# Batch 1's landmark sums around batch 0's z, the A of batch 0's last tokens ahead of B's scaling, batch 2's scores a slot later, and GpSimd's work in another order

## The chip, the cores and the metric

The kernel runs on one core of a Trainium2 chip. The metric is the device time of one execution in microseconds; the median of three executions of the kernel before is 260.71 us (260.47, 260.71 and 262.13).

## The reference

Nystrom attention over 8 batches of 8 heads (576 tokens of 64 values), followed by a SiLU feed-forward layer:

```python
m = 32
scale = 1.0 / np.sqrt(D)
q_lm = q.reshape(B, H, m, S // m, D).mean(axis=3)
k_lm = k.reshape(B, H, m, S // m, D).mean(axis=3)
...
A = sm(q, k_lm)
Bm = sm(q_lm, k_lm)
C = sm(q_lm, k)
Z = Bm.transpose(0, 1, 3, 2) / (norm_1(Bm) * norm_inf(Bm) + 1e-06)
for _ in range(6):
    Z = 2 * Z - Z @ Bm @ Z
return A @ Z @ C @ v
...
h = x @ w_in          # x: 4608 x 512, w_in: 512 x 2048
g = h * (1.0 / (1.0 + np.exp(-h)))
return g @ w_out      # w_out: 2048 x 512
```

Here `sm(a, b)` is a softmax over the last axis of `scale * a @ b.T`, and `norm_1` and `norm_inf` stand for the two matrix norms in the original (written there with numpy's `linalg.norm`).

## The kernel before

Batches run one after the other in a loop over `b`, and each has 16 slots `s`. In a slot TensorE computes one up-projection pair (`l1_mm`, tile `hps`: 256 of the 2048 hidden features for half the tokens), ScalarE applies Silu to it (`l1_act`, tile `gT`), and TensorE works off some down-projection products (`l2_mm`, tile `ops`); how many is written by hand in the lists `CNT` (batches 0 to 2) and `REST`. Between these the attention of the next batch is prepared, so that the feed-forward layer of one batch hides the attention of the following one. The order of every instruction is the order of the Python text: there is no scheduler, and each engine (TensorE PE, VectorE DVE, ScalarE ACT, GpSimd POOL, and the DMA queue SP) works its instructions strictly in that order.

The attention of a batch goes through these steps, each with its helper:

- `load_qk` and `load_v` issue the loads from GpSimd's queue (tiles `nat` with four parts, k and q of heads 0 to 3 and of heads 4 to 7, and `v`). Weights `w_in` and `w_out` are loaded on the same queue.
- Landmark sums over 18 tokens each: for batches 0 and 1 as 18 accumulating products with the identity (`landmarks_pe`, tile `lmp`, evacuated by ScalarE in `landmarks_out`); from batch 2 on by GpSimd (`landmarks_pool`, L223 to L238: five additions for a half of the heads). The result `lmn` is transposed on VectorE (`lm_t`, tile `lmc`).
- `transpose_qk` turns q and k on VectorE (1.25 us each, four for each batch).
- Scores of B and C (`b_scores`, `c_scores`, tiles `bb` and `scp`), their maxima on VectorE, exponentials on ScalarE; B's scaling (`f_mm`, `b_scale`, `f_out`) and then the Newton steps, each a product on TensorE (`ns_mm`) and an update on VectorE (`ns_step`); `x_out` is the last update.
- `w_mm` and `w_out` form C times v, `z_mm` and `z_out` multiply with z, and `m_unit` or `m_pair` multiply the result with `w_in` (tile `mb`), one "unit" for 512 of the 2048 features. So the up-projection of a batch uses `mb` and the transposed A (`AT`) alone.
- The A scores: in batches 0 and 1 chunk by chunk (`a_scores`, `a_exp`, `a_norm`, whose multiplication is GpSimd's, and `a_transpose`); from batch 2 on for the whole batch (`a_pair`: 32 products into `sa`, two transposes and two maxima on VectorE, a subtraction of the maximum on GpSimd, tile `xs`), normalised in `a_sum` and `a_mul`, turned in `a_back`.

The exponential and Silu need different ScalarE tables, so that each switch (`table`) costs a load of 1.28 us.

Where the change lies: before the loop the z of batch 0 is formed (`a.z_mm`, `a.z_out`), then 18 landmark products of batch 1 are issued in two pieces around unit 0. In slots 0 to 4 of batch 0 the rest of batch 1's attention is started and A of batch 0's last tokens is computed; in slots 5 to 15 (`r = s - d`, with `d = 2`) come batch 1's Newton steps, z and units. In batch 1 itself `d` says in which slot batch 2's A scores are made: slot `d` starts batch 2's landmark transpose and `a_pair`, slot `d + 1` the scores of B and C, slot `d + 2` their exponentials, and so on to the units in slots `d + 11` and `d + 13`. `l1_tail` copies a batch's last 64 tokens in front of the next one's, on GpSimd.

PSUM is split in pools: two slots for `hps`, `scp`, `sa` and pairs of units (`ps2`), two for `ops` (`pso1`), one for `bb` and `lmp` (`psn1`), one more (`psa1`). A tile of a pool waits until the tile that had its place has been read.

Of the kernel before, what the change touches and what calls it, by code (L numbers as in the profile page):

```python
# [9 lines left out]
BF = mybir.dt.bfloat16  # L10
# [33 lines left out]
def kernel(  # L44
# [38 lines left out]
    def ps2(nm):  # L83
        return psh.tile([128, 2, 512], FP, tag="h", name=nm)
# [159 lines left out]
    class Att:  # L244
# [376 lines left out]
        def a_pair(self):  # L621
            self.a_first()
            for i in range(2):
                self.a_scores(i)
            for i in range(2):
                nc.vector.transpose(  # L626
                    out=self.xs[:, i],
                    in_=self.sa[i][:, :, 0:HF].rearrange("p r (t n) -> p r t n", n=L))
            for i in range(2):
                nc.vector.tensor_reduce(out=self.nm[:, i], in_=self.xs[:, i], op=OP.max,  # L630
                                        axis=AX.X, negate=True)
                nc.gpsimd.tensor_tensor(  # L632
                    out=self.xs[:, i], in0=self.xs[:, i],
                    in1=self.nm[:, i].unsqueeze(3).to_broadcast((128, 2, SEG // 2, L)),
                    op=OP.add)
# [198 lines left out]
    def l2_add(b, *blocks):  # L834
        for i in blocks:
# [3 lines left out]


    CNT = {0: [0, 0, 0, 0, 4, 4, 2, 4, 4, 4, 2, 2, 2, 2, 1, 1],
           1: [2, 2, 6, 4, 10, 8, 0, 0] + [4] * 8,
           2: [8, 4, 12, 12, 3, 3, 2, 2, 3, 3, 3, 3, 3, 2, 2, 7]}
    REST = [3, 4, 12, 12, 3, 2, 2, 2, 4, 4, 4, 3, 3, 3, 3, 8]

# [71 lines left out]
    load_w_out(2)  # L917
    load_w_out(3)
    load_v(1)
    at = ps2("atp")  # L920
    a.z_mm(at[:, 1, :])
    a.z_out()
    lp = psn1("lmp")
    landmarks_pe(1, lp, 0, 2, (0, 3))

    def first_tokens():
        a.a_transpose(0, at[:, 0, :].bitcast(BF))
        a.a_out(nc.vector.tensor_copy)
        landmarks_pe(1, lp, 0, 2, (3, SEG))

    a.m_unit(0, nc.vector.tensor_copy, nc.scalar.copy, parts=2, between=first_tokens)

    ready = None
    for b in range(B):
# [3 lines left out]
        a0 = a  # L940
        a, ready = ready, None

        d = 2 if b < 2 else 0

        def l1(s):
            h[s] = l1_mm(b, s)
# [4 lines left out]
        for s in range(NDC):  # L951
# [2 lines left out]
                a0.m_pair(a0.m_done)  # L954
            if s <= d and b == 0:
                l1(s)
                act(s)
                if s == 0:
                    landmarks_out(1, lp, 0, 2)
                    a0.m_unit(1, nc.scalar.copy, nc.scalar.copy)  # L960
                elif s == 1:
                    idle(lp[:, 256:512], 8, 256)
                elif s == 2:
                    landmarks_pe(1, lp, 2, 2)
                    landmarks_out(1, lp, 2, 2)
                transpose_qk(1, ORD[s])
# [5 lines left out]
            elif not nxt or s <= d:  # L972
                l1(s)
                act(s)
                n = cnt[s]
                if b == 1 and s == d:
                    a = Att(2)
                    a.lm_t(0, 2)
                if nxt and s == d and not a.early:
                    l2_mm(3)  # L980
                    n -= 3
                    a.a_pair()
                l2_mm(n)

            elif s == d + 1:
# [31 lines left out]
            elif s == d + 2:  # L1017
# [26 lines left out]
            elif b == 0:  # L1044
                l1(s)
                r = s - d
                n = cnt[s]
                if r == 3:
                    nc.vector.tensor_tensor(out=parity, in0=mask[:, 0:2, 0],
                                            in1=mask[:, 2:4, 0], op=OP.add)  # L1050
                    a.ns_mm()
# [4 lines left out]
                elif r == 4:  # L1056
                    a.ns_mm()
                    a.c_transpose(1)
                    a.ns_step()
                    a0.a_norm(2)  # L1060
                    a.c_out(1)
                elif r == 5:
                    act(s)
                    a.ns_mm()
                    a.ns_step()
                    l2_mm(2)
                    n -= 2
                    load_v(2)
                    a.w_scale()
                    a0.a_transpose(1)  # L1070
                    a0.a_out(nc.scalar.copy)
                    a.a_norm(0)
                elif r == 6:
                    a.ns_mm()
                    a.ns_step()
                    act(s)
                    l2_mm(2)
                    n -= 2
                    a.ns_mm()
                    load_qk(3, (1, 0))  # L1080
                    a.a_norm(1)
                    a.ns_step()
                    load_qk(3, (3, 2))
                elif r == 7:
                    a.ns_mm(last=True)
                    act(s)
                    a.x_out()
# [4 lines left out]
                    a.a_norm(2)  # L1092
# [58 lines left out]
            elif s == d + 10:  # L1151
                l1(s)
                a.z_mm()
                a.z_out()
                act(s)
                l2_mm(cnt[s])
            else:
                l1(s)
                act(s)
                if s in (d + 11, d + 13):  # L1160
                    a.m_pair(s - d - 11)
# [6 lines left out]
            if s == 0 and b % 2:  # L1168
                l1_tail(b)
            if b == 0:  # L1170
                if s == 4:
                    load_qk(2)
            elif b + 2 < B:
# [10 lines left out]
                if s == 13 and b > 1:  # L1184
                    ready = Att(b + 2)
                    ready.lm_t(0, 2)
                ts = (7, 8, 10, 12) if d == 0 else (7, 9, 10, 12)
                if s in ts:
                    transpose_qk(b + 2, ORD[ts.index(s)])
                if s == 15 and b == 1:  # L1190
                    ready = Att(b + 2)
                    ready.lm_t(0, 2)
            if nxt and b and s in (9 + d, 14):
                a.a_back((9 + d, 14).index(s))
            if (b, s) == (0, 3):
                l2_add(0, 0)
            elif s == 7:
# [32 lines left out]
```

## Time and profile before

| What | Value |
|---|---|
| Executions | 260.47, 260.71, 262.13 us |
| Profiled execution | 262.13 us, its span 260.4 us |
| Granted TensorE clock, mean | 0.991 |
| HBM read and written | 36.70 and 9.44 MB |

The span is the time from the first to the last instruction of the profiled execution; what lies outside it is 1.7 us. Starts in a timeline count from the beginning of the span. A bracket behind a row gives the idle time before it and what ended that. The costliest groups by engine, each with its count, its busy time and the mean of one:

```profile
L80 PE MATMUL ops<-w_out_sb,gT 128*128 128x512 bf16 (+1 forms) x592 | 146.8, 374 | 0.0
L804 ACT ACTIVATE gT<-hps 128x576 bf16<-128x576 f32 (+2 forms) x128 | 82.6, 652 | 57.2 <-PE hps L80 56.4
L80 PE MATMUL hps<-AT,mb 128*128 128x288 bf16 (+2 forms) x512 | 82.9, 286 | 1.7 <-ACT gT L804 1.0
...
L203 DVE STREAM_TRANSPOSE qkT<-nat 128x576 f32<-128x576 f32 x32 | 39.3, 1244 | 0.3
...
L229 POOL TENSOR_TENSOR lma<-nat 128x1152 f32<-128x1152 bf16 x12 | 28.5, 2377 | 0.0
```

Matmuls overlap, so the mean of one is longer than its share of the time: ten products of 128x512 in a row take 2.33 us. The DMA line of the page lists the issues from GpSimd's queue: 15 loads each of k and q parts (288 KB), 8 of v (576 KB) and 4 each of the two weights (512 KB), besides the two first parts that SyncE loads.

### The profile page before, as it was taken

What the parts mean: (1) busy time and instruction counts of PE and PEld (TensorE: products, weight loads), DVE (VectorE), ACT (ScalarE), POOL (GpSimd) and SP (SyncE); (2) the same over time, 40 slices, a digit from 0 to 9 for tenths busy, and PEclk for the clock granted to TensorE, in tenths of its full rate; (3) what the DMA queues carried; (4) which work ended last, traced back from release to release, by engine and by line L of the source; (5) the groups of instructions that cost most, each with busy time, mean ns of one, the idle gap of its engine ahead of it and who ended that gap; (6) DMA issues with size and microseconds to landing.
All of it is one profiled execution on the core that took longest, in us unless ns stands there. A gap on an engine that the chain in (4) does not pass through costs nothing.

```text
span 260.4 us, 6656 instructions
## 1 busy us (share of the span) xinstructions
PE 249.9 (96%) x2768; PEld 139.0 (53%) x2768; DVE 166.2 (64%) x391; ACT 170.4 (65%) x311; POOL 132.8 (51%) x161
## 2 busy tenths in 40 slices
PE   8989999989899999999999999999999999999994
PEld 2646654454454556456645564545555564556553
DVE  5877876759895969777885788686977745000000
ACT  2276985677847685869575957597668857446511
POOL 7616518993699469845993298138923030100000
PEclk9997999999999999999999999999999999999998
DMA  7999999960529992895279617113621401121122
GB/s 220 195 209 207 207 208 208 224 149 5 141 24 219 228 210 49 115 192 137 55 132 205 110 45 132 42 35 111 107 66 40 120 25 42 41 80 43 42 81 82
DMA packets 30062, 31.16 MB, mean 120 GB/s; under 512 B 10960, under 2 KB 21456, under 8 KB 30032
## 3 DMA queue, kind: packets, MB, share of 16 engines
q0 software_dynamic: 14816, 17.76, 41.4%
q1 hardware_dynamic: 15216, 12.98, 16.7%
q8 instruction: 21, 0.34, 0.5%
q14 instruction: 9, 0.07, 0.1%
HBM read 36.70 MB, written 9.44 MB: 177 GB/s over the span
## 4 chain that ended last, share of the span: by engine, by line
PE 77%; ACT 6%; DVE 6%; POOL 5%; DMA 3%; issue 2%; ACTq 0%; POOLq 0%
PE ops L80 43%; PE hps L80 21%; DMA nat<-in_q_dram 3%; PE bb L80 3%; PE mp L80 2%; PE lmp L80 2%; POOL lma L229 2%; DVE cmx L448 2%; ACT L165 1%; PE sa L80 1%; ACT eC L458 1%; PE wp L80 1%; PE scp L80 1%; ACT ex L644 1%; PE mpp L80 1%
## 5 line engine op out<-in xcount | busy, mean ns | idle before, releaser
L80 PE MATMUL ops<-w_out_sb,gT 128*128 128x512 bf16 (+1 forms) x592 | 146.8, 374 | 0.0
L804 ACT ACTIVATE gT<-hps 128x576 bf16<-128x576 f32 (+2 forms) x128 | 82.6, 652 | 57.2 <-PE hps L80 56.4
L80 PE MATMUL hps<-AT,mb 128*128 128x288 bf16 (+2 forms) x512 | 82.9, 286 | 1.7 <-ACT gT L804 1.0
L80 PEld LDWEIGHTS <-gT 128*128 128x128 bf16 x592 | 53.8, 98 | 48.2 <-issue 9.0
L80 PEld LDWEIGHTS <-mb 128*128 128x128 bf16 x512 | 48.6, 98 | 28.6 <-issue 3.3
L203 DVE STREAM_TRANSPOSE qkT<-nat 128x576 f32<-128x576 f32 x32 | 39.3, 1244 | 0.3
L830 ACT COPY ost<-ops 128x512 f32<-128x512 f32 (+1 forms) x37 | 21.1, 571 | 14.3 <-PE ops L80 14.2
L229 POOL TENSOR_TENSOR lma<-nat 128x1152 f32<-128x1152 bf16 x12 | 28.5, 2377 | 0.0
L407 DVE SCALAR_TENSOR_TENSOR fx<-fx,bb 128x320 bf16<-128x320 bf16 (+1 forms) x39 | 17.0, 435 | 12.5 <-PE bb L80 12.3
L632 POOL TENSOR_TENSOR xs<-xs,nm 128x576 f32<-128x576 f32 x12 | 13.6, 1152 | 21.3 <-DVE nm L630 21.3
L770 DVE CAST mb<-mp 128x512 bf16<-128x512 f32 x28 | 18.0, 684 | 7.4 <-PE mp L80 7.4
L165 ACT ACT_TABLE_LOAD x16 | 20.5, 1283 | 1.1 <-PEq L1214 0.8
L688 POOL TENSOR_TENSOR an<-ex,arec 128x576 bf16<-128x576 bf16 x12 | 13.6, 1158 | 5.3 <-DVE arec L674 5.3
L1126 POOL COPY gate<-wsp 128x2 f32<-128x2 f32 x6 | 1.1, 184 | 28.6 <-DVE wsp L492 28.6
L80 PEld LDWEIGHTS <-fx 32*32 32x32 bf16 (+1 forms) x168 | 8.2, 93 | 12.3 <-DVE fx L407 4.4
L771 ACT CAST mb<-mpp 128x1024 bf16<-128x1024 f32 x14 | 14.2, 1012 | 0.1
L80 PE MATMUL bb<-fx 32*32 32x64 bf16 (+2 forms) x168 | 13.1, 205 | 0.6 <-DVE fx L407 0.3
L626 DVE STREAM_TRANSPOSE xs<-sa 128x576 f32<-128x576 f32 x12 | 8.7, 762 | 6.9 <-PE sa L80 6.9
L234 POOL TENSOR_TENSOR lmc<-lmb,lma 128x384 f32<-128x384 f32 x12 | 12.0, 998 | 0.9
L232 POOL TENSOR_TENSOR lmb<-lma 128x384 f32<-128x384 f32 x12 | 12.0, 996 | 0.9
L448 DVE TENSOR_REDUCE cmx<-scp 128x1 f32<-128x576 f32 x16 | 11.9, 751 | 0.5 <-PE scp L80 0.3
L659 DVE TENSOR_REDUCE arec<-ex 128x18 f32<-128x576 bf16 (+2 forms) x17 | 11.8, 694 | 0.0
(126 smaller groups left out, 263.8 us busy)
## 6 DMA issues: line engine op xcount, KB each, us to landing
out_dram<-ost SPq DMA_DIRECT2D x35, 256.0 KB, 2.0
v<-in_v_dram POOLq DMA_DIRECT2D x8, 576.0 KB, 6.8
nat<-in_k_dram POOLq DMA_DIRECT2D x15, 288.0 KB, 9.3
nat<-in_q_dram POOLq DMA_DIRECT2D x15, 288.0 KB, 10.1
w_in_sb<-in_moe_w_in_dram POOLq DMA_DIRECT2D x4, 512.0 KB, 15.2
w_out_sb<-in_moe_w_out_dram POOLq DMA_DIRECT2D x4, 512.0 KB, 14.1
raw<-in_k_dram SPq DMA_DIRECT2D x1, 576.0 KB, 4.1
raw<-in_q_dram SPq DMA_DIRECT2D x1, 576.0 KB, 5.0
```

The source lines that it names most:

```text
L80: nc.tensor.matmul(out=o, lhsT=lhsT, rhs=rhs, start=start, stop=stop, skip_group_check=True)
L165: nc.scalar.activation(out=spare[:, 1:2], in_=spare[:, 0:1], func=func)
L203: nc.vector.transpose(out=o.rearrange("p (l t) -> p t l", t=SEG), in_=nat_t[b][:, j, :].bitcast(FP).rearrange("p (t l) -> p t l", l=L))
L229: nc.gpsimd.tensor_tensor(out=a1, in0=nat[:, :, 0:3 * w], in1=nat[:, :, 3 * w:6 * w], op=OP.add)
L407: nc.vector.scalar_tensor_tensor(out=n, in0=self.fx, scalar=2.0, in1=self.p, op0=OP.mult, op1=OP.add if self.tiled else OP.subtract)
L448: nc.vector.tensor_reduce(out=mx, in_=self.s[g][:, :, 0:HF], op=OP.max, axis=AX.XY, negate=True)
L632: nc.gpsimd.tensor_tensor(out=self.xs[:, i], in0=self.xs[:, i], in1=self.nm[:, i].unsqueeze(3).to_broadcast((128, 2, SEG // 2, L)), op=OP.add)
L688: nc.gpsimd.tensor_tensor(out=self.an[:, i].rearrange("p r t l -> p (r t) l"), in0=x, in1=r.unsqueeze(2).to_broadcast((128, SEG, L)), op=O ...
L770: nc.vector.tensor_copy(out=o[:, r, 0:512], in_=m[r])
L771: nc.scalar.copy(out=o[:, :, 512:1024], in_=m2)
L804: nc.scalar.activation(out=gT_t[b][:, 2 * s:2 * s + 2, o + c0:o + c1], in_=h[:, :, 0:c1 - c0], func=AF.Silu)
L830: nc.scalar.copy(out=ost[:, 0:hi - lo], in_=st["ps"][:, 0:hi - lo])
```

## The change

Before the loop, eight of batch 1's 18 landmark products now stand ahead of batch 0's z products and four behind them; the transposes of batch 0's A come ahead of unit 0, and the last six landmark products behind it. The sums go to another PSUM pool (`pso1` in place of `psn1`). Unit 1 moves behind the second up-projection, in two halves with the second Silu between them; three of eight idle products are left out.

In slot 4 of batch 0 the Silu table is loaded ahead of unit 2, whose copies go to VectorE, ahead of the transposed C; the A normalisations of batch 0's last tokens stand ahead of B's scaling; and the first Newton product is a slot later. The load of batch 2's v, which was issued in slot 7 behind batch 2's q and k (issued at the end of slot 4), now comes in slot 4 ahead of them and of the two multiplications of A. The loads of batch 3's q and k are spread over slots 5 to 9.

In batch 1, `d` is 3 in place of 2: batch 2's scores and all that follows come a slot later, with new product counts, transposes of batch 3 in slots 8 to 11 (before 7, 9, 10, 12), units in slots 14 and 15 (before 13 and 15) and `a_back` in 12 and 13 (before 11 and 14). From batch 2 on only this differs: the tail copy stands ahead of the subtraction of the maximum (`a_sub`, split off `a_pair`) in odd batches.

```diff
@@ a_pair
                 nc.vector.tensor_reduce(out=self.nm[:, i], in_=self.xs[:, i], op=OP.max,
                                         axis=AX.X, negate=True)
+
+        def a_sub(self):
+            for i in range(2):
                 nc.gpsimd.tensor_tensor(
@@
-           1: [2, 2, 6, 4, 10, 8, 0, 0] + [4] * 8,
+           1: [2, 2, 2, 5, 2, 10, 9, 0] + [4] * 8,
@@ before the loop
     load_v(1)
+    lp = pso1("lmp")
+    landmarks_pe(1, lp, 0, 2, (0, 8))
     at = ps2("atp")
     a.z_mm(at[:, 1, :])
     a.z_out()
-    lp = psn1("lmp")
-    landmarks_pe(1, lp, 0, 2, (0, 3))
-
-    def first_tokens():
-        a.a_transpose(0, at[:, 0, :].bitcast(BF))
-        a.a_out(nc.vector.tensor_copy)
-        landmarks_pe(1, lp, 0, 2, (3, SEG))
-
-    a.m_unit(0, nc.vector.tensor_copy, nc.scalar.copy, parts=2, between=first_tokens)
+    landmarks_pe(1, lp, 0, 2, (8, 12))
+    a.a_transpose(0, at[:, 0, :].bitcast(BF))
+    a.a_out(nc.vector.tensor_copy)
+    a.m_unit(0, nc.vector.tensor_copy, nc.scalar.copy, parts=2)
+    landmarks_pe(1, lp, 0, 2, (12, SEG))
@@ the loop
-        d = 2 if b < 2 else 0
+        d = (2, 3)[b] if b < 2 else 0
+        mp = (11, 13) if d == 0 else (14, 15)
@@ batch 0, slots 0 to 2
                 l1(s)
-                act(s)
                 if s == 0:
+                    act(s)
                     landmarks_out(1, lp, 0, 2)
-                    a0.m_unit(1, nc.scalar.copy, nc.scalar.copy)
+                    lp = psn1("lmp")
                 elif s == 1:
-                    idle(lp[:, 256:512], 8, 256)
+                    a0.m_unit(1, nc.scalar.copy, nc.scalar.copy, parts=2,
+                              between=lambda: act(1))
+                    idle(lp[:, 256:512], 5, 256)
                 elif s == 2:
+                    act(s)
@@ slot d of a batch
+                if s == 0 and b % 2:
+                    l1_tail(b)
                 if b == 1 and s == d:
                     a = Att(2)
                     a.lm_t(0, 2)
-                if nxt and s == d and not a.early:
-                    l2_mm(3)
-                    n -= 3
-                    a.a_pair()
+                if nxt and s == d:
+                    if not a.early:
+                        l2_mm(3)
+                        n -= 3
+                        a.a_pair()
+                    a.a_sub()
@@ batch 0, slot 4
+                table(AF.Silu)
+                a0.m_unit(2, nc.vector.tensor_copy, nc.vector.tensor_copy, pair=True)
                 a.c_transpose(0)
                 a.c_out(0)
-                a0.m_unit(2, nc.vector.tensor_copy, nc.scalar.copy, pair=True)
+                load_v(2)
+                a0.a_norm(1)
+                a0.a_norm(2)
                 a.f_mm()
                 a.b_scale()
                 a.f_out()
                 l2_mm(n)
-                table(AF.Silu)
@@ batch 0, slots 5 to 7
                 if r == 3:
+                    load_qk(3, (1,))
+                    act(s - 1)
+                    a0.m_unit(3, nc.scalar.copy, nc.scalar.copy, parts=2,
+                              between=lambda: act(s))
...
-                    a.ns_mm()
-                    a.ns_step()
-                    act(s - 1)
-                    a0.m_unit(3, nc.vector.tensor_copy, nc.scalar.copy)
-                    a0.a_norm(1)
...
-                    load_v(2)
                     a.w_scale()
-                    a0.a_transpose(1)
-                    a0.a_out(nc.scalar.copy)
-                    a.a_norm(0)
+                    a.a_norm(1)
@@ batch 1
-                ts = (7, 8, 10, 12) if d == 0 else (7, 9, 10, 12)
+                ts = (7, 8, 10, 12) if d == 0 else (8, 9, 10, 11)
...
-            if nxt and b and s in (9 + d, 14):
-                a.a_back((9 + d, 14).index(s))
+            back = (9, 14) if d == 0 else (12, 13)
+            if nxt and b and s in back:
+                a.a_back(back.index(s))
```

The left-out part of the diff moves the transposes of A of batch 0's last tokens, the second transposed C, the A normalisations of batch 1 and the loads of batch 3 within slots 6 to 9, and puts C times v and its evacuation ahead of the last Newton product.

More of the change, by code (lines that the diff above doesn't have):

```diff
@@ L1048 @@
                 if r == 3:
+                    load_qk(3, (1,))
+                    act(s - 1)
+                    a0.m_unit(3, nc.scalar.copy, nc.scalar.copy, parts=2,
+                              between=lambda: act(s))
                     nc.vector.tensor_tensor(out=parity, in0=mask[:, 0:2, 0],
                                             in1=mask[:, 2:4, 0], op=OP.add)
+                elif r == 4:
                     a.ns_mm()
                     a.ns_step()
-                    act(s - 1)
-                    a0.m_unit(3, nc.vector.tensor_copy, nc.scalar.copy)
-                    a0.a_norm(1)
-                elif r == 4:
-                    a.ns_mm()
+                    act(s)
+                    a0.a_transpose(1)
+                    a0.a_out(nc.scalar.copy)
                     a.c_transpose(1)
-                    a.ns_step()
-                    a0.a_norm(2)
                     a.c_out(1)
+                    a.a_norm(0)
+                    load_qk(3, (0,))
                 elif r == 5:
@@ L1065 @@
                     a.ns_step()
-                    l2_mm(2)
-                    n -= 2
-                    load_v(2)
                     a.w_scale()
-                    a0.a_transpose(1)
-                    a0.a_out(nc.scalar.copy)
-                    a.a_norm(0)
+                    a.a_norm(1)
                 elif r == 6:
@@ L1079 @@
                     a.ns_mm()
-                    load_qk(3, (1, 0))
-                    a.a_norm(1)
+                    a.a_norm(2)
                     a.ns_step()
-                    load_qk(3, (3, 2))
+                    load_qk(3, (3,))
                 elif r == 7:
-                    a.ns_mm(last=True)
+                    a.ns_mm()
+                    a.ns_step()
                     act(s)
-                    a.x_out()
                     l2_mm(2)
@@ L1091 @@
                     a.w_out()
-                    a.a_norm(2)
+                    a.ns_mm(last=True)
+                    a.x_out()
+                    load_qk(3, (2,))
                     landmarks_pool(2, 0)
@@ L1159 @@
                 act(s)
-                if s in (d + 11, d + 13):
-                    a.m_pair(s - d - 11)
+                if nxt and s in mp:
+                    a.m_pair(2 * mp.index(s))
                 n = cnt[s]
@@ L1167 @@
                 l2_mm(n)
-            if s == 0 and b % 2:
-                l1_tail(b)
             if b == 0:
```

## The prediction

> **What bounds the kernel now.** I read the page first, then TensorE's waits, then each engine's timeline from 19 to 70 us, where the change lies, then the landing of single loads.
>
> ```profile
> PE 249.9 (96%) x2768; PEld 139.0 (53%) x2768; DVE 166.2 (64%) x391; ACT 170.4 (65%) x311; POOL 132.8 (51%) x161
> ...
> PEclk9997999999999999999999999999999999999998
> DMA  7999999960529992895279617113621401121122
> ```
>
> TensorE is busy 96%, so the end moves only with its idle time, its clock and its work. The loads fill the DMA engines until about 55 us (slices of 6.5 us).
>
> ```profile
> PE hps L80 <- ACT gT L804: 1.0, 1, 1.0
> PE sa L80 <- DVE lmc L271: 0.8, 1, 0.8
> ```
> ```profile
> 20.20:23.50 3.30, 3.19 (x32) 2.50 (x32) 2.19 (x6) 1.47 (x5) 3.30 (x6) 0.50 1.15 205
> ```
> ```profile
> 58.07 0.70 PE L80 MATMUL sa<-qkT,lmc 32*32 32x288 bf16 x32 [0.84 <-DVE lmc L271]
> ...
> 68.19 0.65 PE L80 MATMUL hps<-AT,mb 128*128 128x288 bf16 x4 [0.95 <-ACT gT L804]
> ```
> ```profile
> 46.50 2.38 POOL L229 TENSOR_TENSOR lma<-nat 128x1152 f32<-128x1152 bf16 x1
> ```
>
> The largest stalls after the start stand around batch 2's scores `sa` (58.07) and ten us later (68.19); from 20.2 to 23.5 the granted clock (third figure from the end) is 0.50. The scores wait for VectorE's landmark transpose, and that for GpSimd's two landmark sums, 46.50 to 57.67. The landings, issue plus time to landing:
>
> ```profile
> w_out_sb<-in_moe_w_out_dram POOLq DMA_DIRECT2D x1, 512.0 KB, 16.8
> ...
> v<-in_v_dram POOLq DMA_DIRECT2D x1, 576.0 KB, 18.9
> ...
> nat<-in_k_dram POOLq DMA_DIRECT2D x1, 288.0 KB, 14.3
> nat<-in_q_dram POOLq DMA_DIRECT2D x1, 288.0 KB, 15.2
> ...
> v<-in_v_dram POOLq DMA_DIRECT2D x1, 576.0 KB, 11.6
> ```
>
> In order: last w_out, issued 22.5, lands 39.3; v of batch 1, 23.3, 42.2; first k of batch 2, 29.3, 43.6; first q, 29.9, 45.1; v of batch 2, 39.9, 51.5. Each lands behind the one issued before it, 1.4 us apart for a q or k, 2.9 for v of batch 1. They are served in the order of issue, and the queue never runs dry here.
>
> **The change part by part.** All is set against the profiled execution: 262.13 us, span 260.4, 1.7 outside. It is 1.4 above the median, 260.71.
>
> *Landmark sums around z.* TensorE waits 0.43 us for x (19.76) and 0.31 for the evacuated z (20.31). Twelve sums of 18 (18 took 1.17 us, so 0.06 each) fill both; they go to another PSUM bank, so they need not wait for z. Worth 0 to 0.7; I take 0.4, since the first up-projection then waits for VectorE's copies (0.43 and 0.42). If the added work also keeps the clock up, up to 3.3/2 = 1.65 more; I take 1.4, since one wait on VectorE remains. The two quicker executions lie 1.4 to 1.7 below this one, which fits a full clock in them, though no trace of them is here.
>
> *Unit 1 in halves.* The third up-projection waits for two ScalarE copies (1.10 us); now for two halves (three took 1.07, so 0.72). Worth 0.4 at most; 0.1 once VectorE's four 1.25 us transposes, which follow, set the next wait. Three idle matmuls fewer stand in a wait: 0 (0.3 if not).
>
> *A of the last tokens ahead of B's scaling.* Unit 2's copies go to VectorE (2 x 0.68), so ScalarE's Silu table (1.28 + 0.20) no longer waits for them: 1.0 us earlier. VectorE then has 1.36 + 0.55 (transposed C) + 1.54 (two A norms) + 1.1 (scaling) after 32.95, ready at 37.5 instead of 35.3; the first Newton product, moved a slot later, meets TensorE at about 37.7. So it is covered, by 0.2 us; without cover it costs what is late. TensorE is full there: 0, from -0.3 to +0.6.
>
> These parts bring TensorE to batch 2's scores some 1.4 + 0.4 + 0.1 = 1.9 us sooner, if nothing else holds it.
>
> *GpSimd's order.* v of batch 2 is now issued straight after batch 1's block-diagonal copies (at about 28), and batch 2's four q and k come behind it and behind two A multiplications that wait for VectorE (at about 36 to 38). Their late issue costs nothing, since v of batch 1 holds the queue until 42.2 anyway. Their place does: v of batch 2 is ahead. It takes 2.9 (v of batch 1, the same neighbours) to 3.6 us (its own gap, 47.9 to 51.5); I take 2.9 to 3.2, by the nearer row. The first q lands at 42.2 + 2.9 + 1.45 + 1.45 = 48.0, to 48.7; 48.25 as the value. The Trainium skill ("DMA: Bandwidth & Descriptors", "Anatomy of one DMA") fits a load as 2.0 us plus bytes at 436 GB/s; its variable part for 590 KB is 1.35 us, an estimate by which the sum below would be about 261.7; the trace shows 2.9.
>
> GpSimd itself is free at about 43 to 46, behind an issue that waits for v of batch 2 to land (one issue must wait for the eighth before it, as the fourth q or k at 31.94 waited for w_out). So its sums start on the landing: 46.50 becomes 48.25, and the scores follow at 58.07 + 1.75 = 59.8. Queued behind on VectorE are batch 2's q and k transposes, which now wait for the landings and hold up unit 0's casts of batch 1, and so TensorE's transposes of A, by some 0.7 us.
>
> *Batch 2's scores a slot later.* TensorE gets there at 57.2 - 1.9 + 0.7 + 0.92 (one slot, 55.00 less 54.08) = 56.9. It waits 2.9 us instead of 0.84. From the scores on a chain sets the pace, as in the profile: VectorE's transposes (1.45), maxima (1.37), the C maxima (0.75 each), ScalarE's exponentials (0.74 each, then 1.15), a store copy (0.57), the table (1.28), a Silu, and the up-projection at 68.19, 10.1 us behind the scores. No link of it changes; moved downstream products only fill its gaps. After it, one up-projection more is done than before (0.49 us, 68.19 to 68.67), and the products are equal, 32 and 32.
>
> *The rest.* Batch 3's transposes stand in four successive slots instead of spread: VectorE then has 2.5 us (0.49 + 0.40 + 0.35 + 1.25) in a slot of 1.4, but four more products cover a slot earlier; 0, between -0.3 and +1.2. The later unit pairs: 0, since batch 2 starts some 2.8 us after the first, against 1.3 of copying. The tail copy ahead of the shift in batches 3, 5 and 7 takes 1.03 us and is done by 111.3, while the shift waits for its maximum until 112.67: 0.
>
> **Sum:** +1.75 - 0.49 = +1.26, so 262.13 + 1.26 = 263.4; with 2.9 to 3.6 for v, 263.1 to 263.8. The clock does not enter it: what TensorE gains ahead of the scores it spends in waiting for them.
>
> **The rivals.**
>
> *The loads are not late* (the other side). If q and k of batch 2 land by 43, GpSimd's own 11.2 us end at 54.4, TensorE reaches the scores at 56.2 without waiting, and the chain ends at 66.3 with a slot more done: 68.19 - 66.3 + 0.49 = 2.4 less, 259.7. It decides from a landing before 45. For it: only the order of service argues against it, and that is inferred. Against: every landing in the profile.
>
> *v goes faster.* In their best half microsecond the engines moved 424 GB/s (last figure):
>
> ```profile
> 4.00:4.50 0.50, 0.50 (x3) 0.15 (x1) 0.00 (x0) 0.00 (x0) 0.50 (x1) 1.00 1.12 424
> ```
>
> So 590 KB at that rate would be 1.4 us, the first q lands at 46.5, the scores come 0 to 0.2 later than now: 261.7. Against it: from 6 to 52 us the rate stays near 200. The Trainium skill's 436 GB/s (above) is this rival; its rate is not seen here under load.
>
> *The wait cools the clock.* From 16.8 to 20.2 TensorE was busy 2.56 of 3.41 us, largely with narrow tiles, and the clock fell; from 64.6 to 68.0 it was busy 2.63, with wide ones, and it did not. A wait of 2.9 us may be worse than either. Half speed doubles the links of TensorE in the chain (scores 0.5, up-projection 0.5, C scores 0.6): 1.6 more if all lie inside, nothing if none does; I take 1.1: 264.5, up to 265.0. It hangs on how the wait meets the clock's stretches of 3.4 us. The Trainium skill ("TensorE: Matmul & The Clock Gate", "HAM oscillation") warns of idle gaps over about 3.4 us; by that rule 2.9 alone would not cool, and the time would stay 263.4.
>
> *The change does nothing that counts:* the gate stays at 58.07 with a slot more done: 261.6. The order of GpSimd's issues speaks against it.
>
> **How the numbers follow.** The forecast, 263.4, has 0.48; the cooled clock 0.22; the loads not late 0.13; the faster v and no effect together 0.17. The range 260.9 to 265.0 leaves out the 0.13 and the end of the cooled case. Within 1% of 260.71 (what a measurement can tell) is 258.1 to 263.3. Slower: 0.27 of the forecast's 0.48, since its bounds straddle that edge, and 0.21 of the cooled case: 0.48. Faster needs every stall and the cold stretch gone: 0.04. The rest, 0.48, is the same.
>
> **What would show it.** Right: the first landmark sum on GpSimd starts near 48.2 behind a DMA wait, v of batch 2 lands near 45, `sa` starts near 59.8 after a wait of 2 to 3 us on the landmark transpose, and the up-projection behind the Silu near 69.9. The clock near 20 may be full without moving these. Wrong: landmark sums that start before 46, or `sa` without a wait; then the early gain stays, and the time falls below 260.7.

## The result, and the profile after

The changed kernel takes 264.12 us (median of 11 executions, 263.08 to 264.96) against 260.70 (11 executions of the kernel before, 260.47 to 262.33): 1.0115 of the time before, 95% interval 1.0089 to 1.014. The profiled execution is one of 264.01 us, its span 262.3, against 262.13 and 260.4 before. So it is slower, by 1.2%. Both medians cover two groups of executions. Before, eight lie at 260.47 to 260.75 and three at 262.13 to 262.33. The clocks of these were not recorded, but the experiments ran the kernel before 71 times more, and there it splits the same way: 45 executions at 260.41 to 261.69 with a mean granted clock of 0.997 or more, 25 at 261.88 to 262.59 with 0.991 or 0.992 (one more, of 266.23 at 0.986, is in the slow state and is left out). After, the clock is 0.997 in three executions (263.08 to 263.20) and 0.987 to 0.994 in eight (263.76 to 264.96). The two profiled executions both belong to the group with the lower clock, 0.991 and 0.993. Below, "cold" means that the granted clock is 0.50, and an execution has a "full clock" when its mean is 0.997 or more.

The page of the profile after, its busy times, granted clock and DMA share:

```profile
PE 249.8 (95%) x2765; PEld 138.0 (53%) x2765; DVE 165.0 (63%) x391; ACT 170.4 (65%) x315; POOL 133.4 (51%) x161
...
PEclk9999999997999999999999999999999999999999
DMA  7999999950439991896279726213441411121122
```

TensorE's work is the same within 0.1 us. The dip of the granted clock has moved from the fourth slice (near 20 us) to the tenth (near 62), and the first lull of the loads lies in the same place as before. TensorE's waits:

```profile
PE sa L80 <- DVE lmc L271: 3.8, 2, 3.2
...
PE hps L80 <- ACT gT L807: 0.6, 1, 0.6
PE atp L724 <- DVE mb L773: 0.5, 1, 0.5
```

The wait of batch 2's scores on the landmark transpose has grown from 0.8 to 3.2 us in its longest instance. The third row is the hold on the transposes of A that the prediction put at some 0.7 us; it is 0.5, at 48.73. GpSimd's timeline shows what stands behind the first row:

```profile
27.62 0.78 POOL L114 DMA_DIRECT2D v<-in_v_dram  x1
...
35.73 0.62 POOL L108 DMA_DIRECT2D nat<-in_k_dram  x1
36.35 0.55 POOL L108 DMA_DIRECT2D nat<-in_q_dram  x1
...
45.27 0.53 POOL L108 DMA_DIRECT2D nat<-in_q_dram  x1 [2.30 <-DMA v<-in_v_dram]
48.62 2.37 POOL L229 TENSOR_TENSOR lma<-nat 128x1152 f32<-128x1152 bf16 x1 [2.83 <-DMA nat<-in_q_dram]
```

v of batch 2 is issued at 27.62, ahead of the first q and k. GpSimd has nothing to do from 45.8 to 48.62 but wait for the first q. The issue rows of these three loads, with their time to landing as the last figure:

```profile
v<-in_v_dram POOLq DMA_DIRECT2D x1, 576.0 KB, 17.4
...
nat<-in_k_dram POOLq DMA_DIRECT2D x1, 288.0 KB, 11.1
nat<-in_q_dram POOLq DMA_DIRECT2D x1, 288.0 KB, 12.1
```

So v lands at 45.0, the k at 46.8 and the q at 48.45, where before it was q at 45.1. TensorE's timeline:

```profile
60.15 0.70 PE L80 MATMUL sa<-qkT,lmc 32*32 32x288 bf16 x32 [3.19 <-DVE lmc L271]
...
61.51 0.87 PE L80 MATMUL hps<-AT,mb 128*128 128x288 bf16 x4
...
70.82 0.65 PE L80 MATMUL hps<-AT,mb 128*128 128x288 bf16 x4 [0.56 <-ACT gT L807]
```

The scores come 2.08 us later than before (58.07), the up-projection behind the Silu 2.63 later (68.19). The stretches, with busy time and count of each engine, the granted clock (third figure from the end), the DMA share and GB/s:

```profile
16.70:20.20 3.50, 3.27 (x107) 2.02 (x104) 2.09 (x10) 2.76 (x5) 1.02 (x2) 1.00 1.20 209
20.20:23.60 3.40, 3.18 (x41) 1.81 (x40) 2.92 (x6) 2.54 (x9) 3.40 (x6) 1.00 1.15 206
57.70:61.10 3.40, 0.95 (x34) 0.57 (x35) 0.74 (x2) 0.00 (x0) 2.87 (x4) 1.00 0.00 0
61.10:64.50 3.40, 3.28 (x57) 1.33 (x56) 2.80 (x7) 2.06 (x4) 1.67 (x2) 0.60 0.02 5
```

Before, the first of these stretches reads:

```profile
16.70:20.20 3.50, 2.65 (x94) 1.54 (x93) 2.23 (x11) 2.85 (x5) 1.11 (x2) 0.98 1.21 210
```

At 20 us the clock is now full: TensorE is busy 3.27 of the 3.5 us ahead of it, against 2.65 before. At 58 to 61 it is busy 0.95 of 3.4, and the clock is granted 0.60 in the stretch that follows; that is where the four matmuls of the up-projection at 61.51 take 0.87 instead of 0.65.

The rest of the span is read from the starts of successive batches' scores `sa` (us, batches 2 to 7) and the steps between them:

| | batch 2 | 2 to 3 | 3 to 4 | 4 to 5 | 5 to 6 | 6 to 7 |
|---|---|---|---|---|---|---|
| before | 58.07 | 26.06 | 25.85 | 27.61 | 27.81 | 28.51 |
| after | 60.15 | 26.54 | 25.85 | 27.62 | 27.81 | 27.81 |

After minus before: +2.08 at batch 2's scores, +0.48 in the first step, -0.70 in the last, together +1.86, and the spans differ by 1.9. The prediction put the last one at nothing. Batch 7's scores are made at the end of batch 5, so this last step runs through the slots of batch 5; the expectations below name it after those, "batch 5 to 6", and "batch 5" in them means what is done in the slots of batch 5, which is the attention of batch 6.

### The profile page after: what moved, and what is told of

Same layout as the page of the kernel before. It is cut to its first block, busy times and chain, and to the rows that moved or that the text cites. A ratio compares the mean times of both kernels' runs of the same rounds, so it can differ in the third digit from the quotient of the medians.

```text
span 262.3 us, 6655 instructions
## 1 busy us (share of the span) xinstructions
PE 249.8 (95%) x2765; PEld 138.0 (53%) x2765; DVE 165.0 (63%) x391; ACT 170.4 (65%) x315; POOL 133.4 (51%) x161
## 3 DMA queue, kind: packets, MB, share of 16 engines
q0 software_dynamic: 14816, 17.76, 41.4%
HBM read 36.70 MB, written 9.44 MB: 176 GB/s over the span
## 4 chain that ended last, share of the span: by engine, by line
PE 73%; POOL 11%; DVE 5%; DMA 5%; issue 3%; ACT 1%; POOLq 0%; ACTq 0%
PE ops L80 40%; PE hps L80 19%; DMA nat<-in_q_dram 5%; POOL lma L229 4%; PE idle L80 3%; PE bb L80 2%; PE lmp L80 2%; PE sa L80 2%; POOL lmb L232 2%; POOL lmc L234 2%; PE mp L80 1%; PE scp L80 1%; DVE cmx L448 1%; POOL nat L108 1%; PE mpp L80 1%
## 5 line engine op out<-in xcount | busy, mean ns | idle before, releaser
L80 PEld LDWEIGHTS <-lmc 32*32 32x32 bf16 x576 | 6.3, 91 | 10.5 <-DVE lmc L271 5.2
```

Of the source, the lines that this page charges most:

```text
L80: nc.tensor.matmul(out=o, lhsT=lhsT, rhs=rhs, start=start, stop=stop, skip_group_check=True)
```

## The experiments

The theory is that v of batch 2, placed ahead of its q and k, makes GpSimd's landmark sums late, and with them the whole chain. The rival is that something else in the new GpSimd or TensorE order does it.

**v behind q and k again**, the changed kernel otherwise:

```diff
@@ batch 0, slot 4 (after)
-                load_v(2)
                 a0.a_norm(1)
...
                     load_qk(2)
+                    load_v(2)
```

> The changed kernel with one line moved: v of batch 2 is issued behind batch 2's q and k instead of ahead of them. If the place of v in the load queue is the cause: the first q lands near 45.2 instead of 48.4, GpSimd's landmark sums start at 45.3 to 46.2 instead of 48.62, the scores sa at 56.8 to 57.7 instead of 60.15, TensorE waits under 1 us there, the clock stays full, and the time is 260.0 to 261.2 us. Rival (the slot that comes later, VectorE's transposes in four successive slots or the reordered A work cost the time): 262.8 us or more, with the scores early and new waits behind them.

Measured: 259.43 us (7 executions, 259.19 to 259.6), 0.9924 of before (0.9897 to 0.9952). A repetition on another chip, on which two of the experiments below ran too, gave 259.31 (259.09 to 259.47), 0.9936 (0.991 to 0.9961):

> The changed kernel with v of batch 2 loaded behind batch 2's q and k once more, beside the two that follow on the same chip: 259.4 us, within 0.3, and in batch 5 VectorE's scaling of B's maxima (L304) takes 0.17 us. If the chip used for the other runs was what made e6 slower, the time here lies near 260.2 instead.

The timelines of the first of the two, of GpSimd and of TensorE:

```profile
44.69 2.36 POOL L229 TENSOR_TENSOR lma<-nat 128x1152 f32<-128x1152 bf16 x1 [0.68 <-DMA nat<-in_q_dram]
```
```profile
56.25 0.70 PE L80 MATMUL sa<-qkT,lmc 32*32 32x288 bf16 x32
...
66.37 0.65 PE L80 MATMUL hps<-AT,mb 128*128 128x288 bf16 x4 [0.74 <-ACT gT L807]
```

One load put behind four others takes 4.7 us off the median of the changed kernel (3.7 off its executions with a full clock), and it is then faster than the kernel before as well. The multiplications of A still stand ahead of q and k here, which are issued at 35.38 and 36.00, six us later than before, and yet q lands at 44.6: as predicted, the late issue costs nothing, and the place of v does. The time came out 0.6 below the range expected; the missing term is the tail copy, which the prediction had put at nothing (below). GpSimd still waits 0.68 us for q, but TensorE reaches the scores without a wait (its row has no bracket).

**v ahead, in the kernel before:**

```diff
@@ batch 0 (before)
                 if s == 4:
+                    load_v(2)
                     load_qk(2)
...
                 elif r == 5:
-                    load_v(2)
```

> The kernel before with one line moved: v of batch 2 is issued ahead of batch 2's q and k. If the place of v is the cause: the first q lands near 48.3, the sums start there, the scores come at 59.8 to 60.2 instead of 58.07, and the time is 263.8 to 265.0 us (one slot less is done at the scores than in the changed kernel, so it should be some 0.5 us slower than that). Rival (the order of loads is hidden): 260.5 to 262.2 us as before.

Measured: 265.41 (6 executions, 263.29 to 266.39), ratio 1.0139 (1.0097 to 1.0181). The profiled one, of 263.29:

```profile
47.61 2.38 POOL L229 TENSOR_TENSOR lma<-nat 128x1152 f32<-128x1152 bf16 x1 [0.88 <-DMA nat<-in_q_dram]
```
```profile
59.18 0.70 PE L80 MATMUL sa<-qkT,lmc 32*32 32x288 bf16 x32 [1.79 <-DVE lmc L271]
```

The same move alone makes the kernel before slower, past the changed kernel. The median lies 0.4 above the range expected. The profiled execution lies 0.5 below it, one of two near 263.5 beside four at 265.4 to 266.4: its q lands at 47.5, and its scores come 1.1 us later than before. In it the clock is cold near 20 us; in a second profiled execution, below, it is cold behind the wait.

**The wait filled**, to keep the clock up: 13 idle products of 512 columns ahead of `a_pair` in batch 1 of the changed kernel.

```diff
                         n -= 3
+                        if b == 1:
+                            idle(psa1("fill"), 13, 512)
                         a.a_pair()
```

> The changed kernel with 13 idle products of 512 columns (2.8 us) ahead of batch 2's scores, inside the wait of 3.2 us. If that wait cools the clock and the cooled stretch costs 0.5 us or more behind the scores: sa stays at 60.1, the granted clock stays 1.00 up to 70 us, the up-projection behind the Silu comes 10.1 us after sa instead of 10.7, and the executions lie together at 263.0 to 263.6 instead of 263.1 to 265.0. Rival (the clock does not count there, or the spread has another cause): median 264.1 and the same spread.

Measured: 263.42 (6 executions; four from 263.26 to 263.42, at a mean clock of 0.999 or 1.0; 264.45 at 0.999 and 265.32 at 0.993), ratio 1.0096 (1.0062 to 1.0131). The profiled one is that of 264.45, about 1 us late from its first landmark sum onwards, so that only distances within it are used: `hps` follows `sa` by 10.12 us, and the step from batch 2 to 3 is 25.82, against 10.67 and 26.54 in the changed kernel. That is the price of the cold clock there, 0.55 in the chain and 0.72 in the step. The four quick executions lie some 0.2 above the changed kernel's three at 0.997 (263.08 to 263.20): filling the wait buys back the clock and nothing else.

**The two kernels with v ahead once more**, one more profiled execution each, for the clock:

> The changed kernel once more, for a second profile. Its executions lie at 263.1 to 263.2 with a granted clock of 0.997 and at 263.8 to 265.0 with 0.987 to 0.994. If the clock alone parts them: a time under 263.3 comes with a full clock and 10.1 us from the scores to the up-projection behind the Silu; a time above comes with a half clock behind the scores and 10.6 us or more. In both the scores stay at 59.6 to 60.6.

> e2_v_ahead once more, for a second profile. Its executions lie at 263.3 to 263.6 and at 265.4 to 266.4. If the higher ones are those in which the clock falls at batch 2's scores instead of at 20 us: such a profile shows a granted clock of 0.50 for 3.4 us from about 58 to 62 us, a wait of some 3 us at the scores and more than 10.1 us from the scores to the up-projection behind the Silu. One at 263.3 to 263.6 shows it at 20 us again.

Measured: 263.94 and 265.2, with a mean clock of 0.993 and 0.994. The scores waited 3.38 and 4.17 us, and the step from batch 2 to 3 took 26.95 and 27.41, where kernels with the same instructions and a full clock took 25.82 (the filled wait) and 26.06 (v ahead in the kernel before): 1.1 and 1.35 us more, in executions that are cold behind the wait. In the first of them not all of it is TensorE's half speed. Its scaling of B's maxima, on VectorE, takes 1.10 us beside GpSimd's two subtractions, where the first profile of the changed kernel has 0.23:

```profile
62.34 2.27 POOL L635 TENSOR_TENSOR xs<-xs,nm 128x576 f32<-128x576 f32 x2 [2.10 <-DVE nm L630]
```
```profile
63.55 1.10 DVE L304 TENSOR_SCALAR bbs<-bmx 128x2 f32<-128x2 f32 x1
```

The up-projection behind the Silu comes 11.24 us after the scores here, against 10.67 there. The products of the C scores end 0.25 later after `sa`, the C maxima behind the scaling start 0.59 later; so about 0.3 us, an estimate from these two figures, is this scaling and not the clock. Why it takes so long is seen in the experiments on the tail copy.

**The early part alone**, the landmark sums around z and unit 1 in halves, in the kernel before:

```diff
@@ before the loop, and slots 0 to 2 of batch 0, as in the change
+    landmarks_pe(1, lp, 0, 2, (0, 8))
     at = ps2("atp")
...
+    landmarks_pe(1, lp, 0, 2, (8, 12))
```

> The kernel before with the first parts of the change alone: the landmark sums around z and unit 1 in halves. If the landing of batch 2's first q (45.1) holds the scores to 56.6 at the earliest whatever TensorE gains: 260.2 to 260.7 us, and no execution near 262.2, since the clock stays full at 20 us. Rival (TensorE's gain of 0.4 to 0.9 us reaches the end): 259.7 to 260.1 us.

Measured: 260.4 (12 executions, 260.13 to 260.99), ratio 0.9963 (0.9944 to 0.9983). All twelve have a mean clock of 0.997 or more, where 25 of 70 executions of the kernel before have 0.991 or 0.992. TensorE's timeline has the scores at 56.41, 1.66 before the profiled kernel before, and still waiting:

```profile
56.41 0.70 PE L80 MATMUL sa<-qkT,lmc 32*32 32x288 bf16 x32 [1.06 <-DVE lmc L271]
```

So the early part does what was claimed for it: the profile has no cold stretch at 20 us, no execution has the lower mean clock, and it brings 0.3 us besides, against the median of the 45 full-clock executions of before, 260.68.

**Batch 2's scores in the old slot**, the rest as in the first experiment:

```diff
@@ batch 1
-        d = (2, 3)[b] if b < 2 else 0
-        mp = (11, 13) if d == 0 else (14, 15)
+        d = 2 if b < 2 else 0
+        mp = (11, 13) if d == 0 else (13, 15)
...
-           1: [2, 2, 2, 5, 2, 10, 9, 0] + [4] * 8,
+           1: [2, 2, 6, 4, 10, 8, 0, 0] + [4] * 8,
```

> The kernel of e1_v_behind with batch 1 scheduled as before the change (batch 2's scores in slot 2, old product counts, transposes, units). If the landing gates the scores and the chain of 10.1 us behind them sets the pace, the scores stay at 56.2 to 56.5, TensorE waits 1.0 to 1.4 us there instead of 0.5, and only the one up-projection that is no longer done ahead is lost: 259.43 + 0.49 = 259.9 us, 259.7 to 260.2. Rival (the later slot costs time through VectorE's four successive transposes): 259.3 or less.

Measured: 259.82 (12 executions, 259.45 to 260.33, and one of 263.42 at 0.985), ratio 0.995 (0.993 to 0.997). The scores stay, at 56.07 after a wait of 0.79. The step from batch 2 to 3 is 26.06, against 25.79 with the later slot. Between the medians the slot is worth 0.4 to 0.5; in the traces 0.27.

**The tail copy behind the subtraction again**, in batches 3, 5 and 7; the rest as in the first experiment:

```diff
-                if s == 0 and b % 2:
-                    l1_tail(b)
                 if b == 1 and s == d:
...
                 l2_mm(n)
...
+            if s == 0 and b % 2:
+                l1_tail(b)
             if b == 0:
```

> The kernel of e1_v_behind with GpSimd's tail copy behind the subtraction of the maximum again in batches 3, 5 and 7. If GpSimd has the time there (the copy takes 1.03 us, the maximum comes 1.4 us later): 259.43 us, within 0.2. Rival (the order was worth something in the steady batches): over 259.7 or under 259.2.

Measured: 260.18 (12 executions, 259.71 to 260.4), ratio 0.996 (0.9941 to 0.9979): a miss by 0.75, and the last step is 28.52 again instead of 27.81. The timelines of GpSimd, VectorE and ScalarE in this kernel:

```profile
165.86 2.27 POOL L635 TENSOR_TENSOR xs<-xs,nm 128x576 f32<-128x576 f32 x2 [5.68 <-DVE nm L630]
168.07 1.04 POOL L811 COPY gT<-gT 128x1024 bf16<-128x1024 bf16 x1
```
```profile
168.09 1.04 DVE L304 TENSOR_SCALAR bbs<-bmx 128x2 f32<-128x2 f32 x1
169.05 0.74 DVE L448 TENSOR_REDUCE cmx<-scp 128x1 f32<-128x576 f32 x1
```
```profile
169.23 0.29 ACT L311 ACTIVATE pb<-bb,bbs 128x32 f32<-128x32 f32 x1 [0.34 <-DVE bbs L304]
```

And in the repetition of the first experiment, which has the copy ahead:

```profile
163.33 1.04 POOL L811 COPY gT<-gT 128x1024 bf16<-128x1024 bf16 x1 [3.21 <-ACT gT L807]
165.80 2.27 POOL L635 TENSOR_TENSOR xs<-xs,nm 128x576 f32<-128x576 f32 x2 [1.43 <-DVE nm L630]
```
```profile
168.03 0.17 DVE L304 TENSOR_SCALAR bbs<-bmx 128x2 f32<-128x2 f32 x1
168.26 0.76 DVE L448 TENSOR_REDUCE cmx<-scp 128x1 f32<-128x576 f32 x1
```

An instruction on two values per partition takes 1.04 us when it starts 0.02 us behind a GpSimd copy of 1.04 us, and 0.17 when it starts in the last 0.04 us of GpSimd's subtraction and no copy follows. It scales B's maxima, the exponentials wait for it, and the second row of VectorE, the C maxima, starts 0.96 us after it instead of 0.23. Whether the coincidence is the cause was tried from two sides.

**The tail copy ahead, in the kernel before, and nothing else** (the subtraction is issued in slot `d` after it):

```diff
+        def a_sub(self):
+            for i in range(2):
                 nc.gpsimd.tensor_tensor(
...
+                if s == 0 and b % 2:
+                    l1_tail(b)
```

> The kernel before with one thing changed: the subtraction of the maxima split off A's reductions and put behind the tail copy, which goes ahead (batches 3, 5, 7 change places; the subtractions of the other batches are issued a slot later). If GpSimd's tail copy holds VectorE's scaling of B's maxima in batch 5, that instruction takes 0.17 us instead of 1.04, the step from batch 5's scores to batch 6's takes 27.8 us instead of 28.5, and the time is 0.7 us below before: 260.0, 259.8 to 260.2, against full-clock runs of before at 260.5 to 261.0. If the order of these two costs nothing, as predicted, it is before's time, 260.5 to 261.0.

Measured: 260.03 (12 executions; ten from 259.77 to 260.18 and two of 261.4 to 261.5 at 0.992), ratio 0.997 (0.9947 to 0.9993), the scaling 0.17 us, the last step 27.81. It is the part of the change that pays most, alone.

**The scaling on ScalarE**, with the copy behind the subtraction as in the miss:

```diff
-            nc.vector.tensor_scalar(out=self.bbs, in0=bmx, scalar1=s2, scalar2=None, op0=OP.mult)
+            nc.scalar.mul(self.bbs, bmx, s2)
```

> e6, with the tail copy behind the subtraction as in the kernel before, but the scaling of B's maxima done by ScalarE instead of VectorE. GpSimd's copy runs at the same moment in batch 5 as in e6. If it was VectorE's instruction that was held by the copy, ScalarE's is not: it takes about 0.2 us, the step from batch 5 to 6 comes back to 27.8 us, and the time to e1's, 259.3 to 259.8. If the copy itself, or its place in GpSimd's order, delays batch 5 in another way (batch 5's subtraction later, say), the step stays at 28.5 and the time at 260.0 to 260.4.

Measured: 263.89 (263.61 to 264.36), outside both expectations. ScalarE works in order, and the scaling, which waits for the maxima, now stood ahead of the load of the exponentials' table. ScalarE's timeline:

```profile
60.24 0.20 ACT L304 ACTIVATE bbs<-bmx 128x2 f32<-128x2 f32 x1 [0.73 <-DVE bmx L298]
60.47 1.28 ACT L165 ACT_TABLE_LOAD   x1
```

The table load, which had hidden that wait, is put on the chain: five steps of 26.44, 26.61, 28.36, 28.56 and 28.56, each 0.6 to 0.8 above those of the first experiment. The last is no longer than the one ahead of it, but a delay of 0.75 could hide one of 0.7; so the test was made again.

**The scaling on ScalarE, behind the table load:**

```diff
         def b_exp(self):
...
+            if not self.mean:
+                nc.scalar.mul(self.bbs, self.bmx, s2)
```

> As e8, but ScalarE's scaling of B's maxima stands behind the load of the exponentials' table, where ScalarE no longer waits for the maxima ahead of it, so that table load is again done in the wait. If that order was what made e8 slow, each batch takes about 0.1 to 0.2 us longer than in e1 (ScalarE's 0.20 us instruction on the way to the exponentials), instead of 0.75; if VectorE's held scaling was what made batch 5 longer in e6, batch 5 to 6 takes what batch 4 to 5 takes, within 0.05, and the time is 259.8 to 260.6. If batch 5's 0.70 us came from anything else that GpSimd's order does, batch 5 to 6 is 0.7 us longer than batch 4 to 5 here too, and the time is 260.5 to 261.3.

Measured: 259.81 (10 executions, 259.52 to 260.24), ratio 0.9934 (0.991 to 0.9957). GpSimd and ScalarE:

```profile
168.45 1.04 POOL L813 COPY gT<-gT 128x1024 bf16<-128x1024 bf16 x1
```
```profile
169.19 0.19 ACT L309 ACTIVATE bbs<-bmx 128x2 f32<-128x2 f32 x1
169.41 0.29 ACT L313 ACTIVATE pb<-bb,bbs 128x32 f32<-128x32 f32 x1
```

The copy again comes right behind the subtraction, ScalarE's instruction runs beside it in its usual 0.19 us, and the last two steps are 27.89 and 27.89. So it was VectorE's scaling, held for the length of GpSimd's copy.

The copy is not the only one that holds it. In all twelve traces with the scaling on VectorE, two of its six instances start 0.2 us or more ahead of the end of one of GpSimd's subtractions, and end 0.02 to 0.03 us behind it, long or short: in batch 2's attention they take 0.43 or 0.44 us as a rule, 0.36 in the second profile with v ahead alone, 0.23 in the changed kernel and 1.10 in its second profile, and in batch 4's 0.27. In the kernel before, the first of these:

```profile
60.75 1.16 POOL L632 TENSOR_TENSOR xs<-xs,nm 128x576 f32<-128x576 f32 x1 [2.10 <-DVE nm L630]
```
```profile
61.49 0.43 DVE L304 TENSOR_SCALAR bbs<-bmx 128x2 f32<-128x2 f32 x1
```

So the hold ends with the GpSimd instruction, and how long it is depends on when VectorE arrives.

## Why the prediction was right, and where it was not

*GpSimd's order* was the deciding step, and it is shown from both sides: v behind takes 4.7 us off the changed kernel, v ahead makes the kernel before slower. Predicted: v lands near 45, q at 48.25, sums at 48.25 behind a DMA wait, scores at 59.8 after a wait of 2 to 3 us. Measured: 45.0, 48.45, 48.62, and 60.15 after 3.19. The price of v was right (42.0 to 45.0), and v landed 0.35 ahead of the value taken, 45.35 (48.25 less the 2.9 of k and q); the terms for k and q, 1.45 each, were 1.8 and 1.65, and the sums began 0.17 behind the landing. The term +1.75 measures +2.08, and the up-projection behind the Silu, forecast near 69.9, came at 70.82.

The rival that v goes faster reckoned with 590 KB, the bytes that the load writes. It reads twice as many: the 36.70 MB that HBM read are twice the 17.76 MB that the page gives for the bytes moved by GpSimd's queue, and the 1.18 of SyncE's first parts. By the 1180 KB that it reads, v's 3.0 us are 393 GB/s. The 424 GB/s of the best half microsecond were SyncE's float32 loads alone, which write what they read; against that the loads ran at over nine tenths of the best rate, and the rival had little room.

*Landmark sums around z, unit 1 in halves.* Predicted 1.9 us earlier at the scores and swallowed by the wait: shown. Alone they bring the profiled scores from 58.07 to 56.41, of which 1.35 goes with the cold stretch (56.72 in a full-clock trace with before's order up to there).

*Batch 2's scores a slot later.* The term -0.49 is about -0.25 in the traces (a step of 25.79 or 25.82 with the later slot, 26.06 with the old one). Why it is not the whole up-projection was not tried.

*The wait cools the clock* was a rival with a chance of 0.22, and it is the common case: eight of eleven executions, and the one profiled later. It costs the profiled one 0.72 us (1.1 in the later one, with the held scaling; 1.1 was taken). The forecast of 263.4 is near the others, 263.08 to 263.20, but only because the tail copy's gain makes up for what the loads and the slot were short. The chain of 10.1 us behind the scores held wherever the clock did (10.11 to 10.13 in the kernel before and in every experiment with a full clock there and the scaling on VectorE; 10.67 here). The wait was 3.19 us; by the rule on gaps over some 3.4 us of the Trainium skill ("TensorE: Matmul & The Clock Gate", "HAM oscillation"), weighed in the prediction, it would not cool. The trace disagrees: behind this wait the clock fell.

*The rest: the tail copy, 0.* This step was wrong: it measures -0.70, between batch 6's scores and batch 7's. The prediction asked whether GpSimd had time for the copy in its own queue, and that was right. What failed is the neighbour: in the kernel before the copy runs beside VectorE's scaling of B's maxima, once in six batches at the same moment, and the scaling is held 1.04 us. The row was there to be read: that scaling's shortest, median and longest duration of before are 169, 220 and 1040 ns. The Trainium skill ("SBUF — State Buffer", "Who interferes with whom") says that VectorE and GpSimd share a pair of SBUF ports, that a `tensor_scalar` can take it in a two-port mode, and that whichever comes first keeps it for its whole instruction. The traces agree with that: the held instruction ends with the copy, and on ScalarE it is not held.

*Sum.* Predicted +1.26 on the profiled execution. Measured: +2.08 for the loads, -0.24 for the slot, +0.72 for the clock, -0.70 for the tail copy, together +1.86: 263.99, against 264.01 profiled. That two errors of 0.7 cancelled, the clock and the tail copy, was luck; the miss of 0.6 against the forecast of 263.4 is the loads' term (0.33: k and q 0.55 and the start behind the landing 0.17 more, v 0.35 and the way from the sums to the scores 0.04 less) and the slot (0.25). Against full-clock executions of before the loads cost more, 3.4 us (60.15 against 56.72 in a full-clock trace whose order up to there is before's, the one with only the tail copy and the subtraction moved): the cold stretch at 20 us was in the profiled execution of before, and not in most others. With that figure the two full-clock groups come out as well: 3.43 - 0.25 - 0.70 = 2.48, against 2.46 between 263.14 and 260.68.

*The loads are not late* was the right rival for the experiment, though not for the change: 259.7 was its time, 259.3 to 259.4 is what the kernel gives once v is behind again. The first q then lands at 44.6, ahead of the 45 at which it was to decide, and the scores do not wait; that the time agrees so well owes much to the tail copy, without which it is 260.18. The version with v behind, which keeps every other part of the change, is faster than the kernels before and after.

Left open: *A of the last tokens ahead of B's scaling* was not tried alone. In the changed kernel the scores wait for the loads, so a cost of some tenths ahead of them would not be seen. By the other parts, 260.40 less 0.70 and 0.25 to 0.5, the kernel with v behind would take 259.2 to 259.45, and it takes 259.3 to 259.4; so this part can cost or gain little, an estimate. What sets the clock is open too. TensorE's busy share in a stretch of the timeline does not do so alone (last section), and the length of a single gap was not varied by itself.

## What to carry to other kernels

Write down the order of service of a full load queue before an issue is moved, and put first what the next chain needs first; a load with no urgent reader costs its whole transfer when it stands ahead, and one that turns float32 into bfloat16 reads twice the bytes that it writes. Work that an early gain brings forward is worth nothing until the gate behind it opens, and a longer wait may cost the clock as well: here the waits of 3.19, 3.38 and 4.17 us did, one of 1.79 did not. For a step that moves on GpSimd, look at what VectorE does beside it in every batch, and at the longest duration of each small VectorE instruction, not its median alone.

## What the runs showed that was not expected

A VectorE instruction of 0.17 us was held for 1.04 us by a copy on GpSimd that started 0.02 us ahead of it, and that in one of six batches, with 0.70 us on the end of the kernel. In all five traces with the old order and the scaling on VectorE the last step is 28.51 or 28.52 us, in the seven with the copy ahead 27.81 or 27.82. In a kernel whose TensorE is busy 96%, the largest gain of the change came from two instructions that are not TensorE's.

The kernel with v ahead alone lost its clock at 20 us in one profiled execution and at 60 us in the other. Where the stretch at 20 us is kept busy (3.27 of 3.5 us), as in the changed kernel, or 3.16, as in the kernel with the early part alone, the profiles are not cold there, and none of the latter's 12 executions has a mean clock below 0.997; of the kernel before, busy 2.65 of 3.5 there in its profiled execution, 25 of 70 do. But the busy share alone does not decide: with before's order up to there, the kernel with only the tail copy moved was busy 2.53 of the same 3.5 us and stayed at full clock (third figure from the end of both rows):

```profile
16.70:20.20 3.50, 2.53 (x93) 1.51 (x94) 2.40 (x11) 3.02 (x5) 1.29 (x3) 1.00 1.21 210
20.20:23.60 3.40, 3.37 (x49) 2.34 (x49) 2.74 (x5) 2.44 (x9) 3.40 (x5) 1.00 1.15 205
```

What else decides, no run here shows.
